# Two plain items of a gated scan with two feed-forward layers, run as one stretch with three token halves

## The chip, the core and the metric

The kernel runs on one core of a Trainium2 chip. The metric is the device time of one execution in microseconds (us). Engines are named as in the profile: PE is TensorE (its weight loads are PEld), DVE is VectorE, ACT is ScalarE, POOL is GpSimd, SP is SyncE, which here only issues DMAs. Each engine works through its own queue in order, so an instruction that waits holds back all that stand behind it on that engine.

## What is computed

```python
def _attn_ref(x, f_logit, lower_bound):            # x, f_logit: 2 x 6080 x 256
    sig = 1.0 / (1.0 + np.exp(-f_logit))
    f = lower_bound + (1.0 - lower_bound) * sig
    i = 1.0 - f
    for t in range(S):
        h = f[:, t] * h + i[:, t] * x[:, t]
        y[:, t] = h

x = attn_out.reshape(12160, 256)
h = x @ w_in                                        # 256 x 2048
x = (h - np.tanh(h)) @ w_out                        # 2048 x 256, layer 1
h = x @ moe2_w_in
out = np.maximum(0.01 * h, h) @ moe2_w_out          # layer 2
```

The weights come as float64 words; the products are made from float32r pairs, a high part and a low part of each operand, with three of the four cross products.

## The kernel before

**Items.** The tokens are cut into 12 macros of up to 1024, and a macro into two halves of 512. An item is one layer on one macro: (layer 1, macro 0), (layer 1, macro 1), (layer 2, macro 0), (layer 1, macro 2) and so on, 24 in all. The feed-forward width of 2048 is cut into 8 units `u` of 256. The first three items (`NPLAIN = 3`) are plain: an item has 8 units x 4 products, a product being one 128-wide half `j` of a unit on one token half `n`. All later items use a Strassen scheme with seven products a unit, on sums of weight blocks that are made while item 2 runs (`sums_in`).

**A product** is, in this order: `plain` (six matmuls into one PSUM bank, the block bank), `act` on ACT (tanh of the bank), `shrink` on DVE (bank minus tanh; layer 1 only, it reads the bank a last time), `hi` on ACT and `lo` on DVE (the high and the low part of the result), and `emit_B`: six matmuls with `w_out` into the two PSUM banks that sum the item's output for that half. `emit_B` is issued three products later (`LAG = 3`). The PE queue of a plain item thus reads: plain, emit_B, plain, emit_B, each six matmuls of 128x512. One such pair is called a step below; position `s` counts steps from 0, 32 to an item; the first products are also called p1, p2 and so on, p1 at step 0. The block banks rotate over three: `b10`, `b11` and `c11`.

**The first item's weights** are converted from float64 while it runs. `convert` splits this into s0 (absolute value, ACT), s1 and s2 (three DVE operations), s3 (one DVE operation and the ACT copies that are the high parts of `wa` and `wb`), s4, s5 and s6 (the low parts, DVE, and the store to DRAM). The call for a unit converts `w_in` of the next unit (`wa`) and `w_out` of this one (`wb`). Layer 2's weights go the same way during items 1 and 2 (the list `w`).

**The front** of macros 0 and 1 (`first_front`) takes token-major rows: for a half and each of two feature blocks `k`, PE transposes f and x (`turn`, four 128x128 transposes each), ACT makes tanh and an affine map (`s1`, `s2`), DVE a product (`s4`, called v), two scans of 256 (`s5`); `make_forms` then splits the result into high (ACT) and low (DVE). Half 0 of macro 0 is done ahead of everything. Its second half is loaded from ACT's queue, transposed into the four sum banks, and finished in the first positions. Macro 1's halves follow at positions 9 to 24 and 21 to 35, all their transposes through the one bank `c12`.

**What sets the order.** Everything is written out by hand. `put(p, jobs, q)` hangs jobs on positions, and `work(s)` runs those of position s between a product's `shrink` and its `emit_B` (with the `hi` and `lo` of the product before ahead of them). `evacuate` empties the sum banks: `z` copies them for layer 2 (ACT), `o` transposes and stores them (DVE, SP).

## Time and profile before

| | |
|---|---|
| median of 3 runs | 2020.82 us (2019.74 to 2020.99) |
| the profiled execution, its own time | 2020.35 us |
| its span | 2018.6 us |
| mean granted TensorE clock | 0.994 |
| PE busy | 1980.9 us, 98% |
| DVE busy | 1420.2 us, 70% |
| ACT busy | 1206.1 us, 60% |

The span is what the trace covers; the execution's own time is 1.75 us more. Busy PE is time in which a matmul was in flight; matmuls overlap, so a row of the timeline that lasts 0.62 us for two matmuls is followed by the next one after some 0.45. The clock column is 1.00 where the full 2.4 GHz was granted and 0.50 at 1.2 GHz. The chain that ended last is 95% PE.

### The profile page before, as it was taken

To read this page: it belongs to the slowest core of one execution; us is meant where nothing else is said; L and a number is where in the kernel's file an instruction comes from. 1 tells how busy PE (TensorE), PEld (TensorE's weight loads), DVE (VectorE), ACT (ScalarE), POOL (GpSimd) and SP (SyncE) were. 2 spreads that over 40 slices of the span, in tenths; PEclk is the share of its full clock that TensorE was granted. 3 is DMA by queue.
4 is the path that set the end of the run, shared out by engine and by line. 5 is a ranking of instruction groups with operands and counts; after the bars stand their busy time and mean duration, and the time that the engine had idled before them with its cause. 6 is when DMAs were issued, how large, how long until landed. Compare 5 with 4: busy or idle time off the path is not lost.

```text
span 2018.6 us, 24502 instructions
## 1 busy us (share of the span) xinstructions
PE 1980.9 (98%) x8784; PEld 1649.3 (82%) x8784; DVE 1420.2 (70%) x2254; ACT 1206.1 (60%) x2196; POOL 0.7 (0%) x6
## 2 busy tenths in 40 slices
PE   5999999999999999999999999999999999999998
PEld 3778887888888888888888888888888888889887
DVE  6988878876766776776676677677577677666443
ACT  4555656665565666666566566566666656666554
POOL 0000000000000000000000000000000000000000
PEclk7999999999999999999999999999999999999999
DMA  4546878855555453463563555555446356354352
GB/s 156 198 167 230 257 250 257 265 197 160 164 163 163 161 170 148 160 185 144 165 185 144 164 160 159 160 160 162 148 154 184 144 164 180 144 167 170 144 164 87
DMA packets 366730, 348.30 MB, mean 173 GB/s; under 512 B 268880, under 2 KB 273424, under 8 KB 366608
## 3 DMA queue, kind: packets, MB, share of 16 engines
q1 hardware_dynamic: 363920, 343.85, 52.7%
q10 hardware_dynamic: 2688, 2.89, 0.4%
q8 instruction: 69, 1.13, 0.2%
q14 instruction: 53, 0.43, 0.1%
HBM read 309.07 MB, written 37.62 MB: 172 GB/s over the span
## 4 chain that ended last, share of the span: by engine, by line
PE 95%; DVE 2%; DMA 1%; ACT 1%; issue 0%; SPq 0%; ACTq 0%; DVEq 0%
PE acc L490 50%; PE b L433 22%; PE c L433 17%; PE b L446 4%; PE c L446 2%; DMA rawf<-in_f_logit_dram 1%; DVE gl L474 0%; DVE g L464 0%; DMA wb<-wb 0%; DVE y L325 0%; PE acc L298 0%; DVE raw L138 0%; DVE b L127 0%; DVE b L121 0%; ACT b L116 0%
## 5 line engine op out<-in xcount | busy, mean ns | idle before, releaser
L490 PE MATMUL acc<-gh,wb 128*128 128x512 f32 (+1 forms) x3072 | 1040.3, 388 | 1.2 <-DVE o L509 1.2
L490 PEld LDWEIGHTS acc<-gh,wb 128*128 128x128 f32 x3072 | 577.5, 188 | 116.7 <-DVE o L509 1.9
L474 DVE TENSOR_TENSOR gl<-g,gh 128x512 fp32r<-128x512 f32 (+1 forms) x768 | 500.7, 680 | 221.0 <-ACT gh L469 212.7
L490 PE MATMUL acc<-gl,wb 128*128 128x512 f32 (+1 forms) x1536 | 595.6, 388 | 1.0 <-DVE gl L474 1.0
L469 ACT CAST gh<-g 128x512 fp32r<-128x512 f32 (+1 forms) x768 | 444.9, 615 | 83.8 <-DVE g L464 83.8
L433 PE MATMUL b<-xh,wa 128*128 128x512 f32 (+1 forms) x1344 | 492.5, 387 | 0.0
L433 PE MATMUL c<-xh,wa 128*128 128x512 f32 (+1 forms) x1008 | 362.6, 387 | 0.0
L490 PEld LDWEIGHTS acc<-gl,wb 128*128 128x128 f32 x1536 | 288.8, 188 | 58.4 <-DVE gl L474 2.0
L458 ACT ACTIVATE g<-c 128x512 f32<-128x512 f32 (+1 forms) x275 | 156.5, 602 | 247.8 <-PE c L433 226.8
L433 PEld LDWEIGHTS b<-xh,wa 128*128 128x128 f32 x1344 | 252.3, 188 | 49.5
L456 ACT ACTIVATE g<-c 128x512 f32<-128x512 f32 (+1 forms) x261 | 148.7, 600 | 195.0 <-PE c L433 167.4
L433 PE MATMUL b<-xl,wa 128*128 128x512 f32 (+1 forms) x672 | 260.0, 387 | 0.0
L433 PEld LDWEIGHTS c<-xh,wa 128*128 128x128 f32 x1008 | 189.2, 188 | 37.0
L762 DVE TENSOR_TENSOR c<-b,s 128x512 f32<-128x512 f32 (+1 forms) x168 | 115.1, 685 | 116.5 <-PE b L433 114.9
L433 PE MATMUL c<-xl,wa 128*128 128x512 f32 (+1 forms) x504 | 195.0, 387 | 0.0
L464 DVE TENSOR_TENSOR g<-c,g 128x512 f32<-128x512 f32 (+1 forms) x261 | 170.3, 678 | 32.7 <-ACT g L456 29.8
L708 ACT COPY c<-b 128x512 f32<-128x512 f32 (+1 forms) x168 | 94.9, 565 | 131.1 <-PE b L433 131.1
L464 DVE TENSOR_TENSOR g<-b,g 128x512 f32<-128x512 f32 (+1 forms) x123 | 83.9, 682 | 102.1 <-ACT g L456 102.0
L742 DVE TENSOR_TENSOR c<-b,s 128x512 f32<-128x512 f32 (+1 forms) x168 | 116.1, 691 | 56.2 <-PE b L433 31.9
L433 PEld LDWEIGHTS b<-xl,wa 128*128 128x128 f32 x672 | 126.1, 188 | 24.7
L731 ACT COPY s<-c 128x512 f32<-128x512 f32 (+1 forms) x168 | 98.0, 583 | 37.6 <-PE c L433 29.9
L433 PEld LDWEIGHTS c<-xl,wa 128*128 128x128 f32 x504 | 94.6, 188 | 18.5
(86 smaller groups left out, 1188.5 us busy)
## 6 DMA issues: line engine op xcount, KB each, us to landing
wa<-wa SPq DMA_DIRECT2D x168, 896.0 KB, 4.9
wb<-wb SPq DMA_DIRECT2D x192, 512.0 KB, 5.7
wa<-wa SPq DMA_DIRECT2D x24, 512.0 KB, 5.5
wa<-st SPq DMA_DIRECT2D x24, 512.0 KB, 3.8
out_dram<-o SPq DMA_DIRECT2D x176, 64.0 KB, 1.9
rawf<-in_f_logit_dram SPq DMA_DIRECT2D x72, 128.0 KB, 5.7
rawx<-in_x_dram SPq DMA_DIRECT2D x72, 128.0 KB, 3.1
raw<-wa SPq DMA_DIRECT2D x16, 512.0 KB, 6.8
```

The lines of the kernel that those rows point to most:

```text
L433: nc.tensor.matmul(bank[:, :h], wt[:, s, w], xx[:, v, :h], start=start and i == 0, stop=i == 2, skip_group_check=True,)
L446: nc.tensor.matmul(bank[:, :h], wt[:, s, 2 * k + j], xx[:, v[k], :h], start=i == 0, stop=i == 5,)
L456: nc.scalar.activation(g[:, :h], src[:, :h], AF.Tanh)
L458: nc.scalar.activation(g[:, :h], src[:, :h], AF.Prelu, alpha=0.01)
L464: nc.vector.tensor_tensor(g[:, :h], u["src", name][:, :h], g[:, :h], ALU.subtract)
L469: nc.scalar.copy(gh[:, :h], u["g", name][:, :h])
L474: nc.vector.tensor_tensor(gl[:, :h], u["g", name][:, :h], u["hi", name][:, :h].bitcast(F32), ALU.subtract)
L490: nc.tensor.matmul(bank[e][:, :h], w[:, j, s, es], v[:, :h], start=first and i == 0, stop=i == 2, skip_group_check=True,)
L708: nc.scalar.copy(c11[:, :h], b1[:, :h])
L731: nc.scalar.copy(s5[:, :h], c12[:, :h])
L742: nc.vector.tensor_tensor(c12[:, :h], b1[:, :h], s5[:, :h], ALU.add)
L762: nc.vector.tensor_tensor(c22[:, :h], b1[:, :h], s5[:, :h], ALU.add)
```

## The change

Items 0 and 1 become one stretch of 64 steps. After the first eight products (units 0 and 1 on both halves of macro 0) each unit from 2 to 7 takes six products in a row: two halves of macro 0 and the first half of macro 1 (item 1, n = 0). What is left of item 1 follows: n = 1 for units 5 to 7, whose weights are still in SBUF, and then unit 0 and n = 1 for units 1 to 4, whose converted weights are streamed back from DRAM.

For this, the sums of item 1, n = 0 get the banks `c11` and `c12`, so that the block banks of items 0 and 1 rotate over two, `b10` and `b11`, not three. The front of macro 1's half 0 moves to positions 5 to 7, its half 1 to 37 to 44; half 0 transposes into `c11` and `c12`, half 1 takes its transposes' banks out of the same rotation of two (`next_bank`). The second half of macro 0 is loaded after the affine maps of half 0, and transposed after the second product. The conversion's seven or eight jobs become four (`s0`, `high` = s1 and s2, `low` = s3 and s4, `last` = s5 and s6), hung on chosen positions; layer 2's conversions start at 42 and follow each other by 5.25 steps instead of 33 and 6. The evacuations of items 0 and 1 move into the stretch, those of item 2 come one position earlier, and half of the latter use another SBUF pool.

```diff
+        return f0, [s0, high, low, last]
...
+    def next_bank(n=2):
+        taken[0] += 1
+        return (b1s + [c11])[taken[0] % n]
...
         def turn(nm, k):
+            s[nm, k] = banks[nm][k] if banks else next_bank()
...
+    def sums(it, n):
+        if it == 1 and n == 0:
+            return [c11, c12]
+        return acc[(it + n + (it > 1)) % 2]
...
         def o(e):
-            t = op.tile([P, H], F32, tag="o", name="o")
+            if it == NPLAIN - 1 and n == 0:
+                t = sp.tile([P, H], F32, tag="t", bufs=3, name="o")
+            else:
+                t = op.tile([P, H], F32, tag="o", name="o")
...
-        first[1][0](nc.scalar)
-        for nm in "fx":
-            load1(nm, nc.scalar)
-            turn1(nm, 0), turn1(nm, 1)
-        for k in range(KD):
-            front0[k][1]()
-        run(first[0][1][1:5])
-        run([front0[k][i] for i in (2, 3) for k in range(KD)])
-        run(mix(split0[0:4], first[0][1][5:]))
-        order0 = [(u, j, n) for n in range(2) for u in range(2) for j in range(2)]
-        put(1, mix(*front1) + split0[4:8], 4)
+        run(first[0][1][1:2])
...
+        for k in range(KD):
+            front0[k][1]()
+        first[1][0](nc.scalar)
+        for nm in "fx":
+            load1(nm, nc.scalar)
+        run([front0[k][2] for k in range(KD)] + first[0][1][2:3])
+        run([front0[k][3] for k in range(KD)])
+        run(mix(split0[0:4], first[0][1][3:]))
+        order = [(0, u, j, n) for n in range(2) for u in range(2) for j in range(2)]
+        order += [(1, 1, j, 0) for j in range(2)]
+        begin = {}
+        for u in range(2, NU):
+            begin[u] = len(order)
+            order += [(it, u, j, n) for it, n in ((0, 0), (0, 1), (1, 0)) for j in range(2)]
+        order += [(1, u, j, 1) for u in range(NU - 3, NU) for j in range(2)]
+        order += [(1, 0, j, n) for n in range(2) for j in range(2)]
+        order += [(1, u, j, 1) for u in range(1, NU - 3) for j in range(2)]
...
+        put(1, [turn_all] + mix(*front1) + split0[4:8], 4)
+        stages_at((2, 3, 4, 5), first[2][1])
         for u in range(2, NU):
-            put(NS * u - 7, [first[u + 1][0]])
-            put(NS * u - 2, first[u + 1][1], NS * u + 1)
+            put(begin[u] - 8, [first[u + 1][0]])
+            stages_at([begin[u] + i for i in (-3, -2, 0, 1)], first[u + 1][1])
...
-        for half, a in ((0, 9), (1, 21)):
-            load, turn, stages = first_front(1, half, {nm: [c12, c12] for nm in "fx"})
+        for half, (a, b, e) in enumerate(((1, 5, 8), (28, 37, 45))):
+            load, turn, stages = first_front(
+                1, half, None if half else {"f": [c11, c11], "x": [c12, c12]}
+            )
...
-            put(I + 1 + 6 * u - 5, [load])
-            put(I + 1 + 6 * u, jobs, I + 7 + 6 * u)
+            a = begin[NU - 1] + 2 + 21 * u // 4
+            put(a - 5, [load])
+            put(a, jobs, a + 5)
...
-            if it + 1 < NPLAIN:
-                put(base + 2, evacuate(it, 1), base + 3)
-                put(base + 3, evacuate(it, 0), base + 4)
+            if it == 0:
+                put(46, evacuate(0, 0))
+                put(48, evacuate(0, 1))
+            elif it == 1:
+                put(62, evacuate(1, 0))
+                put(67, evacuate(1, 1))
+            elif it + 1 == NPLAIN:
+                put(base + 1, evacuate(it, 1))
+                put(base + 3, evacuate(it, 0))
...
+            bank = next_bank(2 if it < 2 else 3)
```

**DVE at the conversion for unit 2.** In the rows, `g<-b` or `g<-c` is a shrink, `gl` a lo, L120 to L149 are the conversion, and the banks are `b_86` and `b_87` (the block banks), `c_88` and `c_89` (`c11` and `c12`). Before, from the conversion's last two rows on:

```order
L149 SCALAR_TENSOR_TENSOR wa<-raw 128x512
L149 SCALAR_TENSOR_TENSOR wb<-raw 128x2x256
L464 TENSOR_TENSOR g<-c_88,g 128x512
L474 TENSOR_TENSOR gl<-g,gh 128x512
L464 TENSOR_TENSOR g<-b_86,g 128x512
L474 TENSOR_TENSOR gl<-g,gh 128x512
L120 TENSOR_SCALAR b<-b 128x1024
```

The same place in the change:

```order
L149 SCALAR_TENSOR_TENSOR wa<-raw 128x512
L149 SCALAR_TENSOR_TENSOR wb<-raw 128x2x256
L332 SCALAR_TENSOR_TENSOR v<-g,c_89 128x512
L345 SCALAR_TENSOR_TENSOR y<-g,carry,v 128x256
L345 SCALAR_TENSOR_TENSOR y<-g,y,v 128x256
L484 TENSOR_TENSOR g<-b_87,g 128x512
L494 TENSOR_TENSOR gl<-g,gh 128x512
L332 SCALAR_TENSOR_TENSOR v<-g,c_89 128x512
L484 TENSOR_TENSOR g<-b_86,g 128x512
L494 TENSOR_TENSOR gl<-g,gh 128x512
L345 SCALAR_TENSOR_TENSOR y<-g,carry,v 128x256
L345 SCALAR_TENSOR_TENSOR y<-g,y,v 128x256
```

The front of macro 1's half 0 (both v, four scans, and two lo splits that follow) now stands around the shrinks of p7 and p8 and ahead of p9, the first product of item 1.

**PE where half 1 of macro 1 is transposed**, with the products of steps 38 and 39 around it. Before, a piece with a transpose of macro 1:

```order
L446 MATMUL c_88<-xh,wa 128x512 x2
L446 MATMUL c_88<-xl,wa 128x512 x2
L446 MATMUL c_88<-xh,wa 128x512 x2
L298 MATMUL c_89<-ident,rawx 128x128 x4
L490 MATMUL acc_90<-gh,wb 128x512
L490 MATMUL acc_90<-gl,wb 128x512
```

The change:

```order
L466 MATMUL b_86<-xh,wa 128x512 x2
L466 MATMUL b_86<-xl,wa 128x512 x2
L466 MATMUL b_86<-xh,wa 128x512 x2
L318 MATMUL b_87<-ident,rawx 128x128 x4
L516 MATMUL acc_90<-gh,wb 128x512
L516 MATMUL acc_90<-gl,wb 128x512
L516 MATMUL acc_90<-gh,wb 128x512
L516 MATMUL acc_91<-gh,wb 128x512
L516 MATMUL acc_91<-gl,wb 128x512
L516 MATMUL acc_91<-gh,wb 128x512
```

A transpose went to a bank of its own (`c_89`); now it takes one of the two block banks. Step 39's product goes to `b_86` again, and step 40's to `b_87`, after v has read x out of it.

**ACT where item 1's second half of sums is copied out** (`acc00`, `acc01`), just after item 2 began. Before:

```order
L505 COPY z_1892<-acc00_90 128x512
L505 COPY z_1892<-acc01_91 128x512
L458 ACTIVATE g_1909<-b11_87 128x512
L469 CAST gh_1911<-g_1872 128x512
L505 COPY z_1892<-acc10_92 128x512
```

The change:

```order
L531 COPY z_1754<-acc00_90 128x512
L478 ACTIVATE g_1907<-b11_87 128x512
L489 CAST gh_1909<-g_1885 128x512
L116 ACTIVATE b_1913<-raw_1779 128x1024
L531 COPY z_1754<-acc01_91 128x512
```

The two copies stood side by side; now an act, a hi and the absolute value of a conversion (1024 elements) stand between them. On PE, item 2's first sums into `acc00` and `acc01` (the emit_B of step 65) are issued right after step 68's product, whose act this is.

## Rows read from the trace of the kernel before

**Rows 1.** The page: busy us, share of the span and instructions of each engine.
```profile
PE 1980.9 (98%) x8784; PEld 1649.3 (82%) x8784; DVE 1420.2 (70%) x2254; ACT 1206.1 (60%) x2196; POOL 0.7 (0%) x6
```
**Rows 2.** Waits of PE over the span: us in total, times, longest.
```profile
PE c L298 <- DMA rawf<-in_f_logit_dram: 2.4, 1, 2.4
PE c L298 <- DVE v L312: 1.7, 2, 1.0
PE acc L490 <- DVE o L509: 1.2, 3, 0.5
PE acc L490 <- DVE gl L474: 1.0, 3, 0.6
PE c L298 <- ACT g L304: 0.6, 1, 0.6
```
**Rows 3.** Stretches: length, busy us of each engine, granted clock, DMA share, GB/s.
```profile
13.60:20.40 6.80, 5.51 (x21) 5.12 (x22) 3.91 (x7) 1.24 (x2) 0.00 (x0) 0.50 0.62 205
...
40.90:47.70 6.80, 4.73 (x11) 3.58 (x12) 6.73 (x11) 2.24 (x4) 0.00 (x0) 0.50 0.00 0
...
61.79:98.90 37.11, 34.00 (x157) 27.67 (x156) 36.32 (x54) 22.34 (x38) 0.00 (x0) 1.00 0.59 198
98.90:102.30 3.40, 3.40 (x9) 2.66 (x9) 3.40 (x6) 1.11 (x2) 0.00 (x0) 0.51 0.11 45
...
189.25:306.21 116.96, 116.96 (x518) 96.85 (x516) 96.20 (x146) 67.23 (x119) 0.00 (x0) 1.00 0.77 250
```
**Rows 4.** PE timeline: start, length, operation, matmuls, idle before and its releaser.
```profile
18.22 1.20 PE L446 MATMUL b<-xh,wa 128*128 128x512 f32 x2
...
42.97 1.40 PE L446 MATMUL b<-xl,wa 128*128 128x512 f32 x2 [3.43 <-DVE xl L405]
...
47.57 0.72 PE L446 MATMUL c<-xh,wa 128*128 128x512 f32 x2
...
49.06 0.39 PE L490 MATMUL acc<-gh,wb 128*128 128x512 f32 x1
...
58.60 0.61 PE L446 MATMUL b<-xh,wa 128*128 128x512 f32 x2
...
61.79 0.62 PE L446 MATMUL b<-xh,wa 128*128 128x512 f32 x2
...
98.03 0.63 PE L298 MATMUL c<-ident,rawf 128*128 128x128 f32 x4 [2.37 <-DMA rawf<-in_f_logit_dram]
...
306.21 0.39 PE L433 MATMUL b<-xh,wa 128*128 128x512 f32 x1
```
**Rows 5.** DVE timeline, 33 to 50 us: start, length, operation.
```profile
33.97 1.28 DVE L312 SCALAR_TENSOR_TENSOR v<-g,acc 128x512 f32<-128x512 f32 x2
35.17 1.53 DVE L325 TENSOR_TENSOR_SCAN y<-g,y,v 128x256 f32<-128x256 f32 x2
...
38.44 0.68 DVE L120 TENSOR_SCALAR b<-b 128x1024 f32<-128x1024 f32 x1
...
41.03 0.68 DVE L464 TENSOR_TENSOR g<-b,g 128x512 f32<-128x512 f32 x1
...
42.23 1.29 DVE L405 TENSOR_TENSOR xl<-y,xh 128x512 fp32r<-128x512 f32 x2
43.43 0.69 DVE L132 TENSOR_SCALAR raw<-raw 128x1024 int32<-128x1024 int32 x1
...
45.41 0.69 DVE L143 TENSOR_SCALAR raw<-b 128x1024 int32<-128x1024 int32 x1
...
49.94 0.69 DVE L464 TENSOR_TENSOR g<-c,g 128x512 f32<-128x512 f32 x1 [1.44 <-ACT g L456]
```
**Rows 6.** ACT timeline, at three places: start, length, operation.
```profile
15.46 0.62 ACT L401 CAST xh<-y 128x512 fp32r<-128x512 f32 x1 [0.75 <-DVE y L325]
...
49.32 0.60 ACT L456 ACTIVATE g<-c 128x512 f32<-128x512 f32 x1 [2.96 <-PE c L446]
...
219.07 1.14 ACT L116 ACTIVATE b<-raw 128x1024 f32<-128x1024 f32 x1
```

More of the change, by code (lines that the diff above doesn't have):

```diff
@@ L152, in s6, with high, low, last @@
             parts[i][2]()
-        return f0, [s0, s1, s2, s3, s4, s5] + [lambda i=i: s6(i) for i in range(len(parts))]
+        def high():
+            s1(), s2()
+        def low():
+            s3(), s4()
+        def last():
+            s5()
+            for i in range(len(parts)):
+                s6(i)
+        return f0, [s0, high, low, last]
     def conv_in(l, u, dst):
@@ L279, in load_tokens, with first_front @@
             )
-    def first_front(c, half, banks):
+    taken = [0]
+    def next_bank(n=2):
+        taken[0] += 1
+        return (b1s + [c11])[taken[0] % n]
+    def first_front(c, half, banks=None):
         t0, a = macros[c][0], half * H
@@ L312, in s4 @@
             nc.vector.scalar_tensor_tensor(
-                s["v", k], s["g", k], 1.0, banks["x"][k], op0=ALU.subtract, op1=ALU.mult
+                s["v", k], s["g", k], 1.0, s["x", k], op0=ALU.subtract, op1=ALU.mult
             )
@@ L483, in emit_B @@
         gh, gl, w = u["hi", name], u["lo", name], u["wb"]
-        bank = acc[(it + n) % 2]
+        bank = sums(it, n)
         first = (it, n) not in begun
@@ L499, in evacuate @@
         h = m // 2
-        bank = acc[(it + n) % 2]
+        bank = sums(it, n)
         def z(e):
@@ L607, in tile_gated_scan_two_ffn, with turn_all, stages_at @@
+        order += [(1, u, j, 1) for u in range(1, NU - 3) for j in range(2)]
+        I = NS * NU
+        assert len(order) == 2 * I
+        order += [(2, u, j, n) for u in range(NU) for j, n in ((0, 0), (0, 1), (1, 1), (1, 0))]
+        def turn_all():
+            for nm in "fx":
+                turn1(nm, 0), turn1(nm, 1)
+        def stages_at(p, jobs):
+            for f, at in zip(jobs, p):
+                put(at, [f])
+        stages_at((0, 0, 1, 1), first[1][1])
         put(0, [first[2][0]])
-        put(1, mix(*front1) + split0[4:8], 4)
@@ L639, in tile_gated_scan_two_ffn @@
         put(4 * I + 16, [lambda: conv.__exit__(None, None, None)])
-        for it in range(1, len(items) - 1):
+        put(50, make_forms(2), 61)
+        for it in range(2, len(items) - 1):
             base = I * it
@@ new lines, in tile_gated_scan_two_ffn @@
+        keys = [
+            16 + u if it == 2 else 8 + u if it == 1 and (u == 0 or n == 1 and u < NU - 3) else u
+            for it, u, _, n in order
+        ]
+        listed = list(dict.fromkeys(sorted(keys))) + [NPLAIN * NU, NPLAIN * NU + 1]
+        loads_a, loads_b = {}, {}
+        for old, new in zip(listed, listed[3:]):
+            if new >= NU:
+                e = len(keys) - 1 - keys[::-1].index(old)
+                e = max(e, 2 * I + 24) if new >= NPLAIN * NU else e
+                loads_a.setdefault(e, []).append(new)
+                loads_b.setdefault(e + LAG, []).append(new)
@@ new lines, in tile_gated_scan_two_ffn, with rest, later @@
+        us = [[unit(it * NU + v) for v in range(NU)] for it in range(NPLAIN)]
+        todo, rest = [], None
+        for s, (it, v, j, n) in enumerate(order):
+            u, name, key = us[it][v], f"c{2 - j}{n + 1}", keys[s]
+            bank = next_bank(2 if it < 2 else 3)
+            u["wa"] = wa[key]
+            plain(u, bank, name)
+            act(u, name, bank)
+            shrink(u, name)
+            if rest:
+                rest()
+            work(s)
+            def rest(u=u, name=name):
+                hi(u, name)
+                lo(u, name)
+            def later(u=u, name=name, key=key):
+                u["wb"] = wb[key]
+                emit_B(u, name)
+            todo.append(later)
+            if len(todo) > LAG:
+                todo.pop(0)()
+            for key in loads_a.get(s, ()):
+                stream_a(key)
+            for key in loads_b.get(s, ()):
+                stream_b(key)
@@ L711, in tile_gated_scan_two_ffn @@
                 shrink(prev, "c22")
-            elif rest:
+            else:
                 rest()
+                todo.pop(0)()
             work(NS * t)
```

55 lines of the change are left out of this document (10 added, 45 removed).

## The prediction

> **What bounds the kernel now.** The page comes first: PE is busy for 98% of the span [rows 1], so only PE's losses can be won back. The table of stretches says where they are: from 189 us to the first Strassen product at 306 us PE is busy for 116.96 of 116.96 us [rows 3, 4]. That stretch is 43 steps, so a step costs 2.72 us, and plain and emit_B cost 1.36 each. The PE timeline then gives the loss ahead of it. The first product begins at 18.22 and p6 at 47.57 [rows 4]; in between PE does five plain and two emit_B, 9.5 us of work, so 19.8 us are lost, most of it in waits for one chain of DVE work (PE waits 3.43 us for the low part of the second token half before the row at 42.97). From p6 to p11, which begins at 61.79, there is no loss: 47.57 plus five steps and a transpose is 61.6. From p11 to 306.21 the work is 86 plain and 86 emit_B, 233.9 us, and seven groups of four transposes. One group costs 0.47 us: p10 begins at 58.60, p11 3.19 us later, a step is 2.72. That makes 237.2 of 244.4 us; 7.2 are lost. The waits account for 4.7 of it (2.4 for a load, 1.7 for v, 0.6 for a tanh [rows 2]); and after the load's wait of 2.37 us the clock stood at 0.51 for 3.40 us [rows 3, 4], which is 1.7 us of work lost. Some 0.8 stays unexplained. In this stretch DVE is the engine that PE waits for: 36.32 of 37.11 us busy [rows 3].
>
> So three sums decide: the time at which p11 begins, what is lost from there to 306 us, and the change to item 3. All later work is the same instructions in the same order.
>
> **Prices.** On DVE I take the distance between starts [rows 5]: shrink 0.60 and lo 0.60 (the two from 41.03 to 42.23), a split lo 0.60, v 0.60, two scans 1.55, `high` 2.6 (38.44 to 41.03), `low` 2.0 (43.43 to 45.41), `last` 1.8 (0.6 and two low parts). From the end of a plain to its shrink's start there are 0.88 us: p6's plain ends as the emit_B at 49.06 begins, act starts at 49.32, shrink at 49.94 [rows 4 to 6]. The shrink is over 0.69 later, 1.57 after the plain.
>
> **Part 1, up to p11.** The 16 transposes of the second half no longer stand ahead of p1. What is left to wait for is the split copy on ACT, at 15.46 plus 0.62 [rows 6], so p1 starts its second matmul at 16.0, 2.2 us earlier. I follow the DVE queue from there. The clock was at 0.50 from 13.6 to 20.4 and from 40.9 to 47.7, each time after PE had idled [rows 3]; I take as much here. At half clock p1 ends at 18.6, its shrink starts at 19.5, and shrink, high, shrink, lo, low, last (8.2, with 0.6 for hand-overs) end at 28.3. p3 needs the low part in this and ends at 28.7. Then 0.88, shrink, lo, two v (1.28), four scans (3.2), shrink, lo and two split lo (1.2): 37.7. p5 needs the last of these and, again at half clock, ends near 39.1; before, p5's last four matmuls started at 42.97 and it ended at 45.0. PE leads by 6 us here.
>
> The lead is then used up, since the front of the third half stands in the same queue. After p5's split lo come high, shrink, lo, low, shrink, lo, last: 8.8 us, to 46.5. The emit_B of p3 reads a low part made there, so PE, which is through p6 and two transpose groups at 43.6, waits about 2.8 us; this wait is not in the kernel before. p7 ends at 48.9, and with two more groups, emit_B and p8 PE is at 52.5, and after the next emit_B at 53.9. DVE meanwhile does v and two scans, shrink and lo of p7's step, the second v (its tanh and affine map on ACT come after p7's transposes), shrink and lo of p8's (p8's end plus 0.88), two scans, and after a split copy on ACT the last split lo: 57.5. p9 belongs to the third half and needs it; it ends at 58.2, some 3 us late. emit_B, p10, emit_B: p11 begins at 62.3. Both waits are longer than the one of 2.37 us after which the clock fell; one fall costs up to 1.7, part of it while PE would wait anyway, so I add 0.9: 63.2, against 61.79. **+1.4 us.** Bounds: -1.0 if hand-overs overlap and the clock holds, +3.7 if both waits bring a fall.
>
> **Part 2, p11 to item 3.** Removed: the 4.7 us of waits and the 1.7 us of slow clock, -6.4; three of seven transpose groups are already done, -1.4. With six products to a unit DVE owes 6 x 1.2 + 6.4 = 13.6 us for 16.3 of PE, so nothing is late from step 10 to 36. Added are these.
>
> *The transposes of half 1 in the block banks.* Step 40's product needs the bank from which v reads x, and v stands on DVE behind shrink and lo of step 39. After step 39's plain: 0.88 + 0.60 + 0.60 + 0.69, about 2.8 us; PE has an emit_B (1.36) to do. It waits 1.46 us, and again at step 43: +2.9.
>
> *Two banks.* A plain may start when the shrink two steps back is over, 4.08 us after that plain's end (with three banks, 6.8). The shrink takes 1.57, so DVE may be 2.5 us late. A step without conversion work lets DVE catch up 1.5 us; high, low and last in a row put it back by 1.1, 0.5 and 0.3. Alone that is harmless. Only at steps 43 to 45, where two split lo fall on the conversion, is it exceeded: +0.7.
>
> On banks the Trainium skill speaks against the change: the page "Perfetto Trace Analysis", section "Identifying Performance Opportunities", says that a gap which repeats on the engine that should be saturated can mean that there is too little SBUF or PSUM for the next tile, and its "Matmul Optimizations" asks that all eight banks be used. The kernel before shows no such repeated gap, and no run here has two banks; what the rule would make of the time is rival B.
>
> *Item 1's sums.* The second copy out of `acc01` now stands behind act, hi and an absolute value of step 68 on ACT: 0.26 + 0.5 + 0.5 + 1.1 + 0.6, about 3.0 us after the plain's end (the absolute value lasts 1.14, the copy is taken as long as the act at 49.32, 0.60 [rows 6]). The emit_B into `acc01` is due 0.68 us after it. PE waits 2.3 us, as long as the wait that was followed by half clock: +2.3, and half of 1.7, +0.9.
>
> Sum of part 2: -6.4 - 1.4 + 2.9 + 0.7 + 2.3 + 0.9 = **-1.0 us.** Bounds: -5 (v and the copy find idle queues) to +3 (half clock after each wait, some catching up missed). The loads that are moved, and the streamed weights, cost nothing: each is issued at least four steps, 10.9 us, before its use, and no store that waits for DVE stands ahead of it for longer than a step.
>
> **Part 3, into item 3.** PE waits for `o` three times in the span, 1.2 us, and for a `gl` three times, 1.0 [rows 2]. Some 1.4 of these 2.2 us lie just behind 306 us, where item 2 is evacuated, and the rest at other places. An `o` waits there for its SBUF tile, and holds back the `gl` behind it; moving the evacuations ahead by a step and giving two of them another pool should take away most of it. **-1.2**; bounds 0 and -1.4.
>
> **Sum.** +1.4 - 1.0 - 1.2 = -0.8 us. Against the profiled execution's own 2020.35 us (span 2018.6; it lies 0.47 below the median of the runs) that is **2019.6 us**. What the change wins in the second stretch it pays with waits of its own; DVE's total is unchanged, and it is DVE that sets the pace until unit 7 is converted.
>
> **Rivals.**
>
> *A, the lead is kept (faster).* If DVE is through with the third half's front when p9 comes (its scans slip into the time in which shrinks wait for PE), p9's 3 us and the slow clock behind it are not lost, and p11 begins at 59.3, -2.5 instead of +1.4: 2015.7. For it: DVE idles for short spells while PE works at half clock. Against it: the sum above leaves DVE hardly 3 us of idling between 28 and 57 us. 0.24.
>
> *B, two banks are too few (slower).* If DVE is later than 2.5 us at each conversion, not at one, because ACT's casts and DVE's hand-overs add a microsecond to the 1.57, each conversion costs PE the 0.7 us found for the worst place. Of 12 conversions from step 10 to 64 the other 9 or so with three jobs in a row then cost 6.3 us: 2025.9. It decides from a shrink that ends 2.5 us late. For it: DVE has 36.32 of 37.11 us busy with three banks [rows 3]. Against it: the new order spreads the same work over more PE time. 0.10.
>
> *C, the clock (slower).* One fall is counted, in two parts. If the three waits over 2 us and one of those for v each bring a full 1.7 us, the sum grows by 6.8 - 1.8, 5.0: 2024.6; with the longer falls of 6.8 us seen in the start [rows 3] up to 3 more. 0.06.
>
> *D, the third half fills nothing.* If the waits of the start only change place and PE ends where it did, 2020.35. It lies in the forecast's band and can't be told from it by the time, only by the trace.
>
> **How the numbers follow.** A measurement of this kernel can tell about 0.2%, 4.0 us, from no change. The forecast with D has 0.60: nearly all between 2016.8 and 2024.8, so no change. A, with 0.24, mostly counts as faster; B and C, 0.16, as slower. Range: the sum's bounds are -7.4 and +6.7; with A's 2015.7 at one end and B's and C's 2025.9 at the other, half a case left out on each side, I give 2015.0 to 2024.8. Faster 0.24, same 0.60, slower 0.16.
>
> **What would show it.** Right: p5 ends near 39 us and p11 begins near 63; a wait for a conversion's low part in the emit_B of p3, one before p9 for the split lo, two of about 1.5 us for v near step 40, one of about 2.3 for the z copy just after item 2 begins; none for a load of f; the first Strassen product begins near 305. Wrong: p11 before 60, or small waits for shrinks at every conversion.

## The result and the profile after

The changed kernel takes **2030.74 us** (median; 2029.10 to 2031.16), the kernel before 2020.90 in the same comparison: ratio 1.0051, 95% interval 1.0039 to 1.0064. It is slower by about 10 us, and the range of the prediction (2015.0 to 2024.8) does not hold it. The profiled execution took 2029.10 us, with a span of 2027.3. The page's busy line, beside [rows 1]:

```profile
PE 1986.3 (98%) x8784; PEld 1648.7 (81%) x8784; DVE 1420.4 (70%) x2254; ACT 1206.2 (59%) x2196; POOL 0.7 (0%) x6
```

The work is the same. What changed is what PE waits for. Waits of PE in the changed kernel (us in total, times, longest; two larger rows, both of the first 60 us, are left out), beside [rows 2]:

```profile
PE acc L516 <- DMA wb<-wb: 3.4, 1, 3.4
PE b L466 <- DVE wa L149: 2.7, 1, 2.7
PE acc L516 <- DVE wb L149: 2.7, 1, 2.7
PE b L466 <- DVE v L332: 2.5, 2, 1.3
PE acc L516 <- ACT z L531: 2.0, 1, 2.0
PE acc L516 <- DVE gl L494: 1.7, 3, 1.3
PE b L453 <- DVE c L826: 1.4, 1, 1.4
PE b L466 <- DMA wa<-wa: 0.9, 1, 0.9
```

The first row is new, and nothing in the prediction stands for it. PE's timeline in the changed kernel (start, length, operation, matmuls, idle before and its releaser) gives the places, beside [rows 4]:

```profile
38.07 1.05 PE L466 MATMUL b<-xh,wa 128*128 128x512 f32 x2
...
47.45 0.74 PE L516 MATMUL acc<-gh,wb 128*128 128x512 f32 x2 [2.66 <-DVE wb L149]
...
56.38 0.49 PE L466 MATMUL b<-xh,wa 128*128 128x512 f32 x1 [1.38 <-ACT xh L421]
...
63.37 0.62 PE L466 MATMUL b<-xh,wa 128*128 128x512 f32 x2
...
147.38 0.73 PE L466 MATMUL b<-xh,wa 128*128 128x512 f32 x2 [1.25 <-DVE v L332]
...
206.34 0.70 PE L466 MATMUL b<-xh,wa 128*128 128x512 f32 x2 [0.86 <-DMA wa<-wa]
...
225.40 0.47 PE L516 MATMUL acc<-gh,wb 128*128 128x512 f32 x1 [3.40 <-DMA wb<-wb]
...
238.16 0.50 PE L516 MATMUL acc<-gh,wb 128*128 128x512 f32 x1 [2.02 <-ACT z L531]
...
314.95 0.39 PE L453 MATMUL b<-xh,wa 128*128 128x512 f32 x1
...
325.38 0.50 PE L453 MATMUL b<-xh,wa 128*128 128x512 f32 x1 [1.43 <-DVE c L826]
```

p5 ends at 39.1 and p11 begins at 63.37, as forecast. The first Strassen product begins at 314.95, not near 305, and 8.7 us after that of before. So the loss lies between p11 and item 3, above all in the tail of item 1. SP's timeline there (start and length of each issue) and SP's waits for one kind of store from 180 to 235 us (us in total, times, longest) show what stood ahead of the late weight:

```profile
212.27 0.56 SPq L178 DMA_DIRECT2D wa<-st  x1
212.94 0.55 SPq L191 DMA_DIRECT2D wb<-st  x1
213.54 3.86 SPq L287 DMA_DIRECT2D rawf<-in_f_logit_dram  x4
217.44 3.12 SPq L287 DMA_DIRECT2D rawx<-in_x_dram  x4
220.66 0.66 SPq L275 DMA_DIRECT2D wb<-wb  x1
```

```profile
SPq L178 <- DVE st L149: 29.1, 4, 8.0
```

The load of `wb` stood behind a store that waits for DVE, and behind eight token loads that take SP 7.0 us to issue. It was issued at 220.66 and used as soon as it was there, 4.7 us later. Stretches of the changed kernel (columns as in [rows 3]):

```profile
42.30:226.70 184.40, 172.47 (x763) 139.30 (x762) 155.58 (x232) 102.72 (x177) 0.00 (x0) 1.00 0.49 162
...
61.79:98.90 37.11, 37.11 (x165) 30.77 (x164) 31.42 (x47) 19.84 (x35) 0.00 (x0) 1.00 0.33 114
...
210.00:230.00 20.00, 16.48 (x65) 12.82 (x64) 13.39 (x20) 9.39 (x17) 0.00 (x0) 0.92 0.98 286
...
226.70:230.10 3.40, 3.40 (x10) 2.62 (x9) 0.75 (x1) 0.28 (x1) 0.00 (x0) 0.50 1.04 405
```

The first shows the clock at its upper level, 2.4 GHz, from 42 us to just behind the wait for `wb`. The second is what the change set out for: PE has no loss there, where it had 34.00 of 37.11 [rows 3]. The last is the clock at its lower level, 1.2 GHz, behind the wait for `wb`; that step lost 1.46 us more. The third allows another reading: the DMA engines were busy to 0.98, so the load could be late for want of bandwidth.

### The profile page after: what moved, and what is told of

It reads as the page before. It is cut to its first block, busy times and chain, and to the rows that moved or that the text cites. A ratio compares the mean times of both kernels' runs of the same rounds, so it can differ in the third digit from the quotient of the medians.

```text
span 2027.3 us, 24505 instructions
## 1 busy us (share of the span) xinstructions
PE 1986.3 (98%) x8784; PEld 1648.7 (81%) x8784; DVE 1420.4 (70%) x2254; ACT 1206.2 (59%) x2196; POOL 0.7 (0%) x6
## 3 DMA queue, kind: packets, MB, share of 16 engines
q1 hardware_dynamic: 363088, 341.23, 52.2%
## 4 chain that ended last, share of the span: by engine, by line
PE 94%; DVE 4%; DMA 1%; issue 1%; ACT 1%; ACTq 0%; SPq 0%; DVEq 0%
PE acc L516 48%; PE b L453 22%; PE c L453 17%; PE b L466 5%; PE c L516 1%; DVE gl L494 1%; PE c L466 1%; DVE g L484 0%; DVE y L345 0%; DMA wa<-wa 0%; DMA rawf<-in_f_logit_dram 0%; ACT g L476 0%; DVE y L392 0%; DMA wb<-wb 0%; PE b L318 0%
## 5 line engine op out<-in xcount | busy, mean ns | idle before, releaser
L516 PE MATMUL acc<-gh,wb 128*128 128x512 f32 (+1 forms) x3008 | 1018.1, 388 | 8.1 <-DMA wb<-wb 3.4
L516 PEld LDWEIGHTS acc<-gh,wb 128*128 128x128 f32 x3008 | 565.9, 188 | 121.2 <-ACT st L135 3.8
L516 PE MATMUL acc<-gl,wb 128*128 128x512 f32 (+1 forms) x1504 | 583.5, 388 | 1.8 <-DVE gl L494 1.7
L516 PEld LDWEIGHTS acc<-gl,wb 128*128 128x128 f32 x1504 | 283.0, 188 | 59.4 <-DVE gl L494 3.7
L478 ACT ACTIVATE g<-c 128x512 f32<-128x512 f32 (+1 forms) x274 | 156.1, 602 | 246.9 <-PE c L453 227.2
L476 ACT ACTIVATE g<-c 128x512 f32<-128x512 f32 (+1 forms) x240 | 136.9, 602 | 171.0 <-PE c L453 164.2
L484 DVE TENSOR_TENSOR g<-b,g 128x512 f32<-128x512 f32 (+1 forms) x144 | 98.4, 684 | 117.0 <-ACT g L476 116.8
L484 DVE TENSOR_TENSOR g<-c,g 128x512 f32<-128x512 f32 (+1 forms) x240 | 156.1, 678 | 27.4 <-ACT g L476 24.9
L476 ACT ACTIVATE g<-b 128x512 f32<-128x512 f32 (+1 forms) x144 | 85.9, 596 | 88.8 <-PE b L466 82.5
L466 PE MATMUL b<-xh,wa 128*128 128x512 f32 x344 | 111.6, 406 | 16.0 <-ACT xh L421 9.1
```

Source lines behind the costliest of these rows:

```text
L466: nc.tensor.matmul(bank[:, :h], wt[:, s, 2 * k + j], xx[:, v[k], :h], start=i == 0, stop=i == 5,)
L476: nc.scalar.activation(g[:, :h], src[:, :h], AF.Tanh)
L478: nc.scalar.activation(g[:, :h], src[:, :h], AF.Prelu, alpha=0.01)
L484: nc.vector.tensor_tensor(g[:, :h], u["src", name][:, :h], g[:, :h], ALU.subtract)
L516: nc.tensor.matmul(bank[e][:, :h], w[:, j, s, es], v[:, :h], start=first and i == 0, stop=i == 2, skip_group_check=True,)
```

## The experiments

Times are medians, ratios are to the kernel before, each in its own comparison. The table gives three stretches of each profiled execution, from PE's timeline: the start of p11, from there to the last product of item 2 (step 95), and from there to the end of the span. What a step loses is counted from the start of the product before to the start of its own, over the usual 2.72 us; so a wait in the emit_B between the products of steps 65 and 66 is a loss of step 66. Starts that are the same in code differ by up to 1.6 us, by where the clock falls in the first 52 us: in E2, E4 and E9, which begin p11 last, it stands at 0.50 or 0.51 for 3.4 us from 48 us on, in the change it does not.

| kernel | us | ratio (95%) | p11 | p11 to step 95 | to the end |
|---|---|---|---|---|---|
| before | 2020.9 | 1 | 61.8 | 241.7 | 1715.1 |
| the change | 2030.7 | 1.0051 (1.0039-1.0064) | 63.4 | 248.9 | 1715.1 |
| E1 tokens early | 2026.4 | 1.0032 (1.0020-1.0043) | 63.7 | 244.7 | 1715.9 |
| E9 tokens on another queue | 2028.0 | 1.0038 (1.0025-1.0052) | 64.9 | 244.6 | 1715.6 |
| E3 streams first | 2033.4 | 1.0066 (1.0052-1.0080) | 63.7 | 251.2 | 1715.2 |
| E2 copies together | 2027.5 | 1.0036 (1.0024-1.0049) | 64.8 | 244.7 | 1715.5 |
| E4 v first | 2027.2 | 1.0035 (1.0022-1.0047) | 64.9 | 246.1 | 1716.5 |
| E8 these four | 2019.4 | 0.9996 (0.9988-1.0005) | 64.2 | 237.5 | 1715.3 |
| E10 E8 and two more | 2017.8 | 0.9988 (0.9979-0.9996) | 63.6 | 237.7 | 1713.8 |
| E11 sums early | 2028.5 | 1.0042 (1.0030-1.0055) | 64.5 | 247.8 | 1713.9 |
| E5 before, new start | 2016.2 | 0.9980 (0.9971-0.9989) | 58.0 | 240.3 | 1717.4 |
| E6 before, load early | 2020.2 | 1.0002 (0.9993-1.0010) | 60.8 | 241.5 | 1715.2 |
| E7 E5 and E6 | 2017.0 | 0.9986 (0.9978-0.9995) | 58.1 | 240.4 | 1717.0 |
| E12 E5, v first, evacuation | 2014.3 | 0.9971 (0.9960-0.9983) | 58.1 | 241.9 | 1712.9 |
| E13 E5 and evacuation | 2015.3 | 0.9975 (0.9965-0.9985) | 58.2 | 240.3 | 1715.4 |
| E14 before, two banks | 2020.0 | 0.9998 (0.9989-1.0007) | 61.0 | 241.3 | 1715.6 |

Of the runs that edit the changed kernel, only E8 and E10 have intervals that do not overlap the change's own. What E1, E2, E3, E4, E9 and E11 do singly is read from their traces.

### The late weights: SP's queue or full DMA engines?

**E1.** The token loads away from the streamed weights:

```diff
-                at = (base - 4, base + 2)
+                at = (44 if it == 2 else base - 4, base + 2)
```

> The changed kernel with one edit: the eight token loads of macro 2's first half (7.0 us of issuing on SP) stand at step 44 and not at step 60, where weights are streamed. Theory Q (SP's queue): the load of wb that PE waited 3.40 us for in step 66 was issued late, at 220.66, because a store that waited for DVE and these loads stood ahead of it. Without the loads it is issued some 7 us sooner, the wait of 3.40 and the 1.46 us of work lost at half clock behind it are gone, and the first Strassen product comes 4.9 us sooner; the median falls from 2030.7 to about 2025.9, and the wait of 0.86 us for wa in step 60 may go as well (-1.0). Theory W (the DMA engines are full): their share was 0.93 from 189 to 230 us, so the load would be late wherever it stands; the same bytes are moved, part of them 40 us sooner, the wait shrinks by at most a third, and the time stays within 1.5 us of 2030.7.

The wait for `wb` is gone whole, and the median fell by about what theory Q gave. But the gain is not all in one place: now the clock falls behind the wait for the z copy, where it did not in the change. Two stretches of E1:

```profile
210.00:230.00 20.00, 19.89 (x88) 16.14 (x87) 15.95 (x24) 12.33 (x22) 0.00 (x0) 1.00 0.77 286
233.90:237.30 3.40, 3.40 (x9) 2.64 (x8) 0.00 (x0) 0.58 (x2) 0.00 (x0) 0.50 1.17 184
```

What theory W forecast for E1, a wait shorter by at most a third, did not come. But E1 also took load off the DMA engines (0.77 for 0.98), so it does not tell whether SP's queue or full engines held `wb`.

**E9** was meant to: the same loads at the same step, only issued on POOL's queue (`q` is `nc.gpsimd` for macro 2's first half, else `nc.sync`).

```diff
-            nc.sync.dma_start(
+            q.dma_start(
```

> The changed kernel with one edit: the eight token loads of macro 2's first half are issued at the same step 60 as in the change, on POOL's queue and not on SP's. The same bytes at the same time, only SP no longer spends 7.0 us on issuing them. Theory Q (SP's queue): the load of wb is then issued right behind the stores, near 213.5 and not 220.66, and PE's wait of 3.40 us for it goes, with the 1.46 us at half clock behind it; as with the loads at step 44, the clock may fall behind the wait for the z copy instead (1.6), so 3.3 to 4.9 us less: 2025.8 to 2027.4. Theory W (full DMA engines, share 0.98 from 210 to 230 us): the load shares the engines with the same token loads as before, the wait stays at 2 us or more, and the time within 1.5 us of 2030.7.

`wb` is issued at 215.18, right behind the stores, and PE does not wait for it. But the edit did more than its expectation says. POOL's queue holds no other DMA, so POOL issued these loads as soon as their tiles were free, at 52.33 us and not near 213. They also went another way: as 384 packets on a queue of their own, while the queue of SP's loads moved 354,768 packets for 363,088 in the change. POOL and SP in E9, the new queue (packets, MB, share of the DMA engines) and the stretch:

```profile
52.33 3.25 POOL L287 DMA_DIRECT2D rawf<-in_f_logit_dram  x4 [51.03 <-PE c L318]
55.57 3.11 POOL L287 DMA_DIRECT2D rawx<-in_x_dram  x4
...
213.88 0.56 SPq L178 DMA_DIRECT2D wa<-st  x1
214.54 0.55 SPq L191 DMA_DIRECT2D wb<-st  x1
215.18 0.66 SPq L275 DMA_DIRECT2D wb<-wb  x1
```

```profile
q0 software_dynamic: 384, 1.05, 0.2%
```

```profile
210.00:230.00 20.00, 19.89 (x88) 16.15 (x87) 15.67 (x24) 12.43 (x23) 0.00 (x0) 1.00 0.85 312
```

So E9, too, took load off the DMA engines from 210 to 230 us (0.85 for 0.98), and it does not decide this either. What E1 and E9 show together is that the token loads between the stores and `wb` make the wait. The store's own wait for DVE does not: before 213 us SP waits 7.5 us for it in E1 as in the change, and `wb` is in time. Whether `wb` was held by the 7.0 us that SP needs to issue the token loads, or by the time that the DMA engines need to move them, no run separates. While they moved, the engines were full at a low rate, share 1.15 for 180 GB/s (from 226.7 to 230.1 us it was 1.04 for 405):

```profile
216.50:221.50 5.00, 4.88 (x22) 3.73 (x21) 2.27 (x4) 3.48 (x6) 0.00 (x0) 1.00 1.15 180
```

For SP's issuing speaks that `wb`, once issued, was there after 4.7 us, where the median of all loads of `wb` in the change is 5.6; and that eight token loads took SP as little to issue here as anywhere in the span (6.9 to 11.4 us). The time of E9 is 0.6 above the forecast's upper end, with p11 1.6 us later than in the change and a fall of the clock behind the z copy.

The Trainium skill, page "DMA: Bandwidth & Descriptors", section "Issuing engines are not separate DMA queues", says that several issuing engines save only issuing time, which is usually small beside the transfer. For one load the trace agrees: SP issues four token loads in 3.12 and 3.86 us, 0.8 to 1.0 us each, and from issue to landing they take 3.1 and 5.7 (medians of `rawx` and `rawf`). But eight in a row are 7.0 us ahead of a load that arrived in 4.7. E9 does not show that issuing time is all that is saved, since its loads also moved in time.

**E3** tried the same by order alone, on SP: streamed loads ahead of a step's stores and token loads, `wb` one step later.

```diff
+            for w_key in loads_a.get(s, ()):
+                if w_key < NPLAIN * NU:
+                    stream_a(w_key)
+            for w_key in loads_b.get(s - 1, ()):
+                stream_b(w_key)
             work(s)
...
-            for key in loads_a.get(s, ()):
-                stream_a(key)
-            for key in loads_b.get(s, ()):
-                stream_b(key)
```

(`wa` of item 3 stays behind `work`.)

> The changed kernel with one edit: in each step of the first stretch the streamed weight loads are issued on SP ahead of that step's other jobs (stores of converted weights and token loads) and not behind them; a load of wb is issued one step later in the order, but ahead of the jobs of that step. The same loads, stores and bytes, nothing taken away. Theory Q (SP's queue): the two late loads (0.86 us for wa in step 60, 3.40 us for wb in step 66) were held by stores that wait for DVE and by token loads, and both waits go or fall below 0.5 each, with the half clock behind the second: 4.5 to 5.9 us, median near 2025.5. Theory W (full DMA engines): the waits stay at 2 us or more in sum and the time within 1.5 us of 2030.7.

The expectation failed, through its edit. The wait for `wa` in step 60 went; but the `wb` in question, a step later, now stands behind the token loads of the step before and a load of `wa` besides. SP's timeline and PE's in E3:

```profile
213.98 3.86 SPq L287 DMA_DIRECT2D rawf<-in_f_logit_dram  x4
217.89 3.13 SPq L287 DMA_DIRECT2D rawx<-in_x_dram  x4
221.12 0.53 SPq L269 DMA_DIRECT2D wa<-wa  x1
221.69 0.60 SPq L275 DMA_DIRECT2D wb<-wb  x1
```

```profile
227.03 0.76 PE L516 MATMUL acc<-gh,wb 128*128 128x512 f32 x1 [5.64 <-DMA wb<-wb]
```

Issued 1.0 us later, it cost 2.2 us more: it also took 0.6 us longer to arrive, and PE was there 0.6 us sooner. What stands ahead in SP's queue sets this wait, in the bad direction too.

### The waits that were forecast

**E2**, both copies at step 67:

```diff
-                put(67, evacuate(1, 1))
+                put(67, evacuate(1, 1), 68)
```

> The changed kernel with one edit: both copies of item 1's second half of sums are put at step 67, so that no act, hi or absolute value of step 68 stands between them on ACT. Theory: PE's wait of 2.02 us for the second copy (238.16) was just these jobs, and it goes to between 0 and 0.3; the step is 2.0 to 2.3 us shorter and the median 2028.5. Rival (DVE sets the pace at that place, and PE's wait stood beside DVE's catching up): what PE wins there it gives back in the wait for gl in step 75 (1.30 us), which grows by one to two us, and the time falls by less than 0.8.

PE's wait for z is gone (step 69 was 2.31 us long over the usual 2.72 in the change, 0 here), and the wait for gl in step 75 stayed at 1.3. The rival falls. The profile is 4.2 us shorter from p11 to step 95, more than these 2.3, since the wait for `wb` was 2.91 us and the clock did not fall behind it.

**E4**, v of macro 1's half 1 (`f[2]`) ahead of the shrink of steps 39 and 42:

```diff
+                if half:
+                    early[(39, 42)[k]] = f[2]
...
+            if s in early:
+                early[s]()
             shrink(u, name)
```

> The changed kernel with one edit: the v of macro 1's second half stands on DVE ahead of the shrink of steps 39 and 42, not behind it and its lo. The prediction put PE's wait for each at 1.46 us (DVE's shrink, lo and v after act); the trace showed 1.25 and 1.25 us, 2.9 us over both steps. Theory: v waits then for nothing but the transposes and its tanh, PE's two waits go and the shrinks, 0.6 us later, wait for no one: 2.5 to 2.9 us less, median 2028.0. Rival (the waits stand beside DVE's own lateness): the shrink moved back makes the next plain or gl late by 0.6 to 1.2, so that half or less is won, under 1.5 us.

Steps 40 and 43 lose 0.0 and 0.05 us for 1.43 and 1.44 in the change: 2.8 us, as the theory has it. The time fell by some 3.2 (0.0016 of 2020), the same within the measurement.

**E8**, the edits of E1 to E4 together:

> The changed kernel with four edits together: token loads of macro 2's first half at step 44, both copies of item 1's second half at step 67, the streamed loads ahead of a step's other jobs, v ahead of the shrink. Theory: each takes away a wait of its own (3.40 and 0.86 for weights with 1.46 at half clock, 2.02 for the copy, 2.5 for v), all of them on PE's path and none covered by another: 10 to 10.8 us less, 2019.9 to 2020.7, the level of the kernel before. If they hide one behind the other (DVE late after all), half of it: near 2025.

11 us less: the four do not hide one another. With the token loads gone from step 60, E3's order does no harm. From p11 to step 95 E8 needs 237.5 us, 4.2 less than the kernel before; but p11 is 2.4 later, and in sum the two kernels take the same time.

### Item 3

**E11**, the sums of item 3's weights where the kernel before has them; the evacuation stays as changed:

```diff
-        a = 2 * I + 20
+        a = 2 * I + 18
```

> The changed kernel with one edit: the sums of item 3's weights begin two steps earlier, as in the kernel before; item 2's evacuation stays as changed. The change's wait of 1.43 us for c at 325.38 stood behind two adds of these sums (0.42 each) and a transpose (0.71) on DVE. Theory S (the sums): 0.9 to 1.4 us of this wait go, and the 0.87 of steps 84 and 85, where the sums begin, with it or to other steps: 1.0 to 2.3 us less, median 2029. Theory E (the evacuation): the transpose alone makes the wait, 0.7 or more of it stays, and the time moves by less than 0.7.

DVE in the change, ahead of the `c` that PE waited 1.43 us for at 325.38, and PE in E11:

```profile
323.25 0.42 DVE L225 TENSOR_TENSOR s<-s,f 128x256 f32<-128x256 f32 x1
323.70 0.42 DVE L226 TENSOR_TENSOR s<-f,s 128x256 f32<-128x256 f32 x1
324.04 0.71 DVE L538 STREAM_TRANSPOSE o<-acc 128x512 f32<-128x512 f32 x1
324.68 0.65 DVE L826 TENSOR_TENSOR c<-b,s 128x512 f32<-128x512 f32 x1
```

```profile
324.67 0.50 PE L453 MATMUL b<-xh,wa 128*128 128x512 f32 x1 [0.64 <-DVE c L826]
```

Both theories were half right: 0.8 of the wait belongs to the two adds, 0.6 to the transpose that the evacuation put there. The stretch behind step 95 is 1.2 us shorter; steps 84 and 85 kept their 0.87. By the time, 2028.5 against 2030.7, the gain cannot be told from none.

**E10**, E8 with E11's edit and macro 2's front two steps later (`base + lead + 2` for `it == 2`):

> The changed kernel with the four edits of the run with all together, and two more: the sums of item 3's weights begin two steps earlier (where the kernel before has them), and macro 2's front two steps later. What was left there: 1.43 us for c in item 3, 0.88 in steps 84 and 85, 1.62 for gl in step 75. Theory: each of these is DVE work standing ahead of what PE needs, and moving it takes 2 to 3.5 us off 2019.4: 2016 to 2017.4. Rival: DVE is full there, the work meets another step's shrink or gl in its new place, and less than 1 us is won.

By the medians 1.6 us less than E8, between theory and rival, but the intervals overlap. In the profile the gain lies behind step 95 (1713.8 for 1715.3), where E11's edit stands. Moving macro 2's front won nothing: the wait for gl in step 75 went, and 1.47 us came back in step 85.

### Parts of the change in the old order

**E5**, the start alone. `lb` goes through SP, the transposes of the second half and its front move behind p2, and the first conversions' parts are spread:

```diff
-        put(0, first[1][1], 2)
+        stages_at((0, 0, 1, 1), first[1][1])
...
-        put(1, mix(*front1) + split0[4:8], 4)
-        put(2, first[2][1], 5)
+        put(1, [turn_all] + mix(*front1) + split0[4:8], 4)
+        stages_at((2, 3, 4, 4), first[2][1])
```

> The kernel before with one part of the change alone: its start (the transposes of the second half behind the first product's, the order of the first conversions), while item 0 still runs two token halves on three block banks and item 1 follows by itself. Theory P (the prediction's part 1): the 6 us by which PE leads at p5 (43 -> 37 us) are lost in the change because the third half's front stands in DVE's queue; without the third half nothing of macro 1 stands there, so the lead is kept up to p11 but for the clock: p11 begins near 56, 4 to 6 us before 61.79, and the median falls from 2020.9 to about 2015.9. Rival R: the lead is lost to DVE in any order, since DVE has to convert each unit (36.3 of 37.1 us busy from 61.8 to 98.9 in the kernel before): then p11 begins sooner, but waits for shrinks and conversions give the time back by step 36, and the median stays within 1 us of 2020.9.

PE's timeline, and a stretch in item 3 of E5:

```profile
58.00 0.62 PE L446 MATMUL b<-xh,wa 128*128 128x512 f32 x2
```

```profile
317.40:320.80 3.40, 3.40 (x10) 2.65 (x8) 3.18 (x5) 0.62 (x1) 0.00 (x0) 0.50 0.91 159
```

p11 begins 3.8 us sooner than before, a little less than theory P has it, and 5.4 sooner than in the change: the lead is kept without the third half, and is used up with it (1.4 of the 5.4 are three transpose groups that PE does ahead of p11 in the change and behind it in E5). Of 5.2 us won at step 95, 2.3 are lost behind it, 1.7 of them to the fall of the clock shown.

**E6**, macro 1's second load four steps earlier (`put(a - 8, ...)` for half 1):

> The kernel before with one edit: the token loads of macro 1's second half are issued four steps earlier. The kernel before waited 2.37 us for one of them (98.03) and then worked 3.40 us at half clock. Theory P: both belong to that load, the time falls by 2.4 + 1.7 = 4.1 us, to 2016.8. Rival R: DVE is behind by then anyway (36.3 of 37.1 us busy), so that PE meets a wait for DVE soon after in place of the load; 1 to 2 us are left of the gain, 2019.5.

The rival holds, and not even its 1 to 2 us are left: the ratio is 1.0002. The wait for the load is gone, and in its place PE waits for DVE. Waits of PE in E6, beside [rows 2]:

```profile
PE c L298 <- DVE v L312: 3.5, 2, 2.8
...
PE acc L490 <- DVE gl L474: 2.0, 4, 1.0
```

The fall of the clock moved too, to 114.7 us behind the wait for v. In the old order these 4.1 us could not be had by themselves.

**E7**, both:

> The kernel before with both edits: the change's start, and the token loads of macro 1's second half four steps earlier. If DVE does not set the pace, the two gains add up: about -9 us, near 2012. If DVE sets it until unit 7 is converted, the sum is hardly more than the larger of the two: 2016 to 2017.

Not additive: from p11 to step 95 E7 takes 240.4 us, E5 240.3.

**E14**, two block banks in items 0 and 1:

```diff
-                u, name, bank = us[v], f"c{2 - j}{n + 1}", hb[s % 3]
+                u, name, bank = us[v], f"c{2 - j}{n + 1}", hb[s % (2 if it < 2 else 3)]
```

> The kernel before with one edit: items 0 and 1 take two block banks in turn and not three, in the old order, the old start and with the old loads. Theory T (two banks leave DVE 2.5 us of lateness and the third bank only hides what DVE owes): DVE is busy for 36.3 of 37.1 us from 61.8 to 98.9 either way, waits of PE change place, and the time grows by less than 2 us. Theory B (rival B of the prediction: each conversion with three jobs in a row is late by 0.7 us at two banks): some 9 conversions, 6 us more, near 2026.5; in the old order, where DVE has less time for each conversion than in the new one, it can be more.

By the time, the third bank is worth nothing that can be measured. E14's stretch, beside [rows 3], has DVE as busy as before, and its largest new wait of PE is for a shrink:

```profile
61.80:98.90 37.10, 34.67 (x159) 27.67 (x158) 36.31 (x53) 21.88 (x37) 0.00 (x0) 1.00 0.58 199
```

```profile
PE b L446 <- DVE g L464: 0.7, 1, 0.7
```

In its steps two banks do have a price, 1.8 us of losses that the kernel before has not. They are made up for by the load, which PE waits 1.58 us for and not 2.37, with no fall of the clock behind it. That is theory T; the 6 us of theory B did not come, so rival B is out for the old order, and in the change itself two banks cost 0.7 us in all (below). The page "Perfetto Trace Analysis" of the Trainium skill (section "Matmul Optimizations") asks that all eight banks be used: E14's 1.8 us go the way of that rule, and no time measured here shows them.

**E12 and E13**, E5 with the change's evacuation of item 2. In E12 v also stands ahead of the shrink, and the first transposes are issued ahead of the last emit_B into the same sums, so these lack a product; the amount of work is the same. E13 has the evacuation alone, behind the last emit_B, which moves ahead with it.

```diff
+            elif it + 1 == NPLAIN:
+                put(base + 1, evacuate(it, 1))
+                put(base + 3, evacuate(it, 0))
...
```

> The kernel before with the change's start, as in the run of that start alone, and two more edits: item 2's evacuation a step earlier with its own tiles for o, as in the change, and v of macro 1's second half ahead of the shrink. The start alone gave 2016.15; left there were 1.56 us for o and gl in item 3, a fall of the clock right behind these (0.50 from 316.8 to 320.2, 1.7 us of work) and 1.75 for v. Theory: the o and gl waits go, and the fall with them, 3.3 us less, near 2012.9; the v wait adds up to 1.7 (2011.2) if DVE is not late there anyway, nothing if it is. Rival: item 3 has the wait for c instead, 1.43 us as in the change, and the clock falls all the same: 2015 to 2016.

> The kernel before with the change's start and with the change's evacuation of item 2 (its last emit_Bs and its transposes a step earlier, tiles of their own for o), nothing else. Theory E: the term of item 3 is real, and the change lost it to the sums that it moved by two steps; here they stay where they were, so the waits for o and gl in item 3 (1.56 us with the start alone) and the fall of the clock behind them (1.7) go: 2016.2 - 3.3, 2012.9; if the fall comes all the same, 2014.6. Rival: the evacuation only swaps these waits for one on c, as in the change: 2016 or more.

In E12 v first does harm. PE waits 2.40 us for a tanh on ACT to free the bank (0.6 in E5), the clock falls there, and from p11 to step 95 it takes 1.6 us more than E13:

```profile
116.99 0.66 PE L298 MATMUL c<-ident,rawx 128*128 128x128 f32 x4 [2.40 <-ACT g L304]
```

In E13 the fall in item 3 is gone, and of E5's 1.56 us of waits for o and gl there is one of 0.63 for c left. Behind step 95 its profile is 2.0 us shorter than E5's, where 3.3 were forecast. By the time, 2015.3 against 2016.2, with intervals that overlap, the gain cannot be told from none. E13 is the best version whose sums are whole: 0.9975 of the kernel before, 0.9924 of the change (0.9975 / 1.0051).

## Why the prediction was wrong, step by step

Against the profiled execution, 2029.1, the sum misses by 9.5 us: 0.2 in part 1, 8.2 in part 2, 1.2 in part 3. The median lies 1.6 above that execution.

- **Part 1 (+1.4): right,** by its own steps. +1.6 measured; p5 ends at 39.1 (39.1 forecast), the emit_B of p3 waits 2.66 us (2.8), p9 comes late for its split, p11 begins at 63.37 (63.2). That the last of these fits to 0.2 is luck in part. p9 ends 1.1 us later than forecast (59.3 for 58.2), its longer waits are for ACT's split copies (1.38 and 0.88) and not for DVE's last split lo, and the 0.9 booked for a fall of the clock did not come in this profile; with a fall at 48 us, in E2, E4 and E9, p11 begins at 64.8 to 64.9. E5 shows the reason to be the one named: without the third half p11 begins at 58.0. So rival A, the lead kept, is what the old order does.
- **Part 2, what is removed (-6.4 - 1.4 + 0.7 for two banks = -7.1): right in sum.** E8 has v, copy and weights out of the way and stands 4.2 below before; its steps 64 to 66, 75, 84 and 85 still lose 3.2 us that the forecast does not have, so -7.4. The two-bank loss was 0.68, where two split lo meet the conversion, as forecast, but in steps 47 to 49 and not 43 to 45. E6 shows that this is a gain of the new order, not of the early load.
- **v (+2.9): right.** 1.43 and 1.44 us in steps 40 and 43; E4 takes out just these.
- **The z copy (+2.3): right,** 2.31; E2. Its fall of the clock (+0.9) was not there in the profile of the change, and was 1.6 in E1, E3, E9 and E11.
- **"The loads that are moved, and the streamed weights, cost nothing": the step that failed.** Steps 60, 66 and 67 lost 1.03 + 3.82 + 1.46 = 6.3 us. It counted the distance from the place in the order to the use, four steps, and held that no store stands ahead for longer than a step. But a unit streamed in the tail of item 1 is used for two steps, not six, so loads come thrice as fast; stores waited up to 8.0 us for DVE; and the eight token loads, which the diff leaves at step 60, took 7.0 us of SP to issue just where the fast loads now stand. E1 and E9, which take the token loads away from there, end the wait for `wb`; E3, which leaves `wb` behind them and behind one more load, makes it longer, and ends the wait for `wa` by issuing it ahead of a step's stores. Whether SP's issuing of the token loads or the DMA engines' moving of them held `wb` stays open.
- **Not priced: DVE between steps 64 and 86.** The conversions of the next layer's weights come every 5.25 steps, and the scans of macro 2's front stand right behind the end of one: gl waits 1.30 us (step 75, 1.59 lost), and 1.3 more in steps 64, 65, 84 and 85. E10 removed the first and got another. Which order would have none stays open.
- **Part 3 (-1.2): the evacuation did it, another line took it back.** The three waits of before (1.43) are gone, one of 1.43 stands in their place; E11 wins 1.2 by the sums that the diff had moved by two steps and the prediction passed over.

Put together, part 2: -7.4 + 2.9 + 2.3 + 6.3 + 1.6 + 1.3 = 7.0, where 7.2 was measured. The share of E1's and E9's gain that the clock took is shown by its rows; why it falls behind one wait and not another is not.

## What to carry to other kernels

Price every DMA that a change moves by what is issued ahead of it on its own queue: the issuing time of each, the time that it takes the DMA engines, and the wait of a store at its head. The distance to the use in steps counts only from the moment of issue. When a DMA is moved to another engine's queue, look in the trace when it ran: on POOL's empty queue E9's loads ran 160 us ahead of where the program has them. And before a wait is booked as a gain, ask what its neighbour owes: with DVE busy for 36.3 of 37.1 us, taking a load's wait away only showed the wait for DVE behind it.

## What the hardware showed unexpectedly

The clock did not follow the length of a wait. After waits for z of 2.02 us it fell to 0.50 for 3.4 us in E1, E3, E9 and E11, and not in the change or in E4. After waits for `wb` it fell in the change (3.40 us) and in E4 (3.09), and not in E2 (2.91) or E11 (2.53), though both are longer than 2.02. In E5 it fell behind three waits of 0.46 to 0.61 us; behind the same three, of 0.33 to 0.60, it held in the kernel before. E11, behind its waits for `wb` (226.16) and for z (237.31):

```profile
226.80:230.20 3.40, 3.40 (x17) 2.77 (x16) 2.25 (x3) 1.34 (x4) 0.00 (x0) 1.00 1.03 407
238.40:241.80 3.40, 3.40 (x10) 2.63 (x9) 0.04 (x1) 1.10 (x2) 0.00 (x0) 0.50 1.09 170
```

PE did 17 records of matmuls in the one stretch and 10 in the other. A single fall, about 1.6 us, is as large as most of the terms of this sum.
